# Two attention blocks in one kernel on one Trainium2 core: quotients taken one per score tile, copies given to an engine by its load, and two q chains ahead of k's first

## The chip, the cores and the metric

The kernel runs on one core of one Trainium2 chip. The metric is the device time of one execution in microseconds (us); lower is better. TensorE (PE) does the matmuls, ScalarE (ACT), VectorE (DVE) and GpSimd (POOL) work on their results, and SyncE (SP) issues the transfers (DMAs). Each engine carries out its instructions in program order and waits where an operand is not ready; matmuls write to PSUM, which is held here in banks of 128 x 512 fp32 numbers.

## What is computed

Two blocks, A and B, each with x of 2048 x 640, wqkv of 640 x 1920 and wo of 640 x 640, all bf16; H = 32 heads of Dh = 20. The two outputs stand side by side.

```python
def _A_ref(x, wqkv, wo):                      # W = 256
    q, k, v = ...                             # x @ wqkv, split by heads
    scores = jnp.einsum("bhqd,bhkd->bhqk", q, k) * (Dh ** -0.5)
    mask = (idx[:, None] - idx[None, :] >= 0) & (idx[:, None] - idx[None, :] < W)
    p = _softmax(jnp.where(mask[None, None], scores, -1e9), axis=-1)
    o = jnp.einsum("bhqk,bhkd->bhqd", p, v)
    return o.transpose(0, 2, 1, 3).reshape(B, S, D) @ wo

def _B_ref(x, wqkv, wo):
    phi = lambda t: jnp.where(t > 0, t + 1, jnp.exp(t)) + 1e-6
    pq, pk = phi(q), phi(k)
    kv = jnp.einsum("bhsd,bhse->bhde", pk, v)
    z = jnp.einsum("bhsd->bhd", pk)
    num = jnp.einsum("bhqd,bhde->bhqe", pq, kv)
    den = jnp.einsum("bhqd,bhd->bhq", pq, z)[..., None] + 1e-6
    return (num / den).transpose(0, 2, 1, 3).reshape(B, S, D) @ wo
```

A is attention over a sliding window of 256 positions. B is linear attention, so its sums over the keys are taken once and the queries then go through a merged weight.

## The kernel before

The 2048 rows are handled in four stripes of 512 (s = 0 to 3). A bank is one PSUM buffer `dense`; there are four, used in turn. The scores have a buffer of their own, `S_ps`, of four banks and only one copy.

**Score tiles.** The main loop runs over 76 score tiles, 16 for stripe 0 and 20 for each other stripe. A tile is: the scores of four heads (L742) into S_ps, a tiny ACT instruction on one element (L736), one exp over 128 x 2048 (L760, ACT), and masks by GpSimd (L773, `affine_select`). Two tiles after a group of four heads is complete, `values` multiplies the probabilities with v into a dense bank (L800); VectorE transposes the result (`T`, L811), and later takes the reciprocal of the row sums and normalises (`rest`, L821 and L827). After a stripe's seventh group four DMAs turn the normalised rows for the output product (L841); its last group adds a small transpose on VectorE (L848).

**Fill.** Between the scores of one tile and the next, TensorE gets other matmuls. All of them are in one list `plan`: `at(t0, t1, gen, n)` spreads n banks of a generator over plan times t0 to t1, and `do` places single actions, DMAs among them. The list is sorted by plan time. `take` draws from it: every tile gives `rate` columns of credit, which is (FILL - TAIL + 32 x VALUES) / 76, and a tile with `values` has VALUES columns taken off. So the plan times fix only the order, and the columns fix how many banks go into a tile.

The fill is, in rough order: q, k and v of A (`a_rows`, `a_v`); B's keys with phi (`b_keys`); the sums over B's keys (`b_sums`, `b_kv`); B's queries with phi (`b_q`); the merge of B's values into its weights (`b_merge`, L649); the denominators (`b_den`, L691 on TensorE, L701 and L702 on VectorE); and the output products of both blocks (`a_out`, `b_out`, through `wo_proj`). Before the loop stand the first v chains, the regrouping of the weights of q and k by copies on three engines (`regroup`, L356, L359, L362), and one chain each of q and k.

**What follows a bank.** A chain is five matmuls into one bank. Then either `evac` copies the bank to SBUF, on ACT (L258) or VectorE (L260), or `phi` works on it: exp on ACT (L285), a minimum on VectorE (L290) and a combination on VectorE that reads the bank again (L293). The two VectorE steps are put into `later`, and are issued two banks on or after the next scores, so a phi bank stays taken until then. DMAs that read a result go through `soon(fn, n)`, which issues them n banks later; `settle()` issues all that are waiting. All of them go through SyncE's one queue.

**B's queries.** `b_q(s)` makes five phi banks. After each, a DMA transpose brings it to rows by tokens (`tok`, L679). `b_den(s)` multiplies all five phi tiles with the key sums. A quotient (`quotients`, L714, VectorE) divides 128 rows of `tok` by their denominators, and a DMA transpose (L718) brings them into `oT_B[s]`, which lives in a buffer named `xA`; `b_out(s)` reads it. `divide(t0, t1, s)` places a stripe's four quotients in the plan.

**Who copies.** Where the caller names no engine, `evac` chooses. Before and after the main loop it takes VectorE and ACT by turns. In the loop `spare` holds ACT's allowance in columns: it is raised by 1200 a tile, up to 1200; a copy of n columns goes to ACT if the allowance is at least n, and takes n + 160 off; each phi exp takes 672 off. What ACT has no allowance for goes to VectorE.

Of the kernel before, what the change touches and what calls it, by code (L numbers as in the profile page):

```python
# [20 lines left out]
SB = 512  # L21
TPS = SB // P

FILL = 398440
TAIL = 13000

VALUES = 2200
SPARE = 1200
COPY = 160

# [58 lines left out]
def kernel(  # L91
# [150 lines left out]
            posts.pop(0)[1]()  # L242


    spare = [None]

    def evac(dst, src, n=SB, to=None):

        if to is None:
            to = "D"  # L250
            if spare[0] is None:
                turn[0] += 1
                to = "AD"[turn[0] % 2]
            elif spare[0] >= n:
                spare[0] -= n + COPY
                to = "A"
        if to == "A":
            nc.scalar.activation(out=dst, in_=src, func=ACT.Copy)  # L258
        else:
            nc.vector.tensor_copy(out=dst, in_=src)  # L260

    turn = [0]

    def bank(wide=False):
        flush(begun[0] - 2)
# [15 lines left out]
    def phi(dst, src, view=lambda t: t[:], then=None):  # L281


        e = ep.tile([P, SB], BF16, name="e")
        nc.scalar.activation(out=view(e), in_=src, func=ACT.Exp)  # L285
        if spare[0] is not None:
            spare[0] -= SB + COPY

        def rest():
            nc.vector.tensor_scalar(  # L290
                out=e[:], in0=e[:], scalar1=1e-6, scalar2=1.0 + 1e-6, op0=ALU.add, op1=ALU.min
            )
            nc.vector.scalar_tensor_tensor(  # L293
                out=dst, in0=src, scalar=0.0, in1=view(e), op0=ALU.max, op1=ALU.add
            )
            if then is not None:
                then()

        later.append((begun[0], rest))
# [361 lines left out]
    pq_of, tok_of, rden_of = {}, {}, {}  # L661

    def b_q(s):
        xt = xB[NS + s]
        pq = pqp.tile([P, KT, SB], BF16, name="phi")
        pq_of[s] = pq
        tok = rp.tile([P, TPS, D], BF16, name="tok")
        tok_of[s] = tok
        for c in range(KT):
            ps = bank()  # L670
            yield from chain(
                ps[:],
                lambda kt: w_sb["B"][:, kt, c * P : (c + 1) * P],
                lambda kt: xt[:, kt, :],
                SB,
            )

            def to_tokens(c=c):
                nc.sync.dma_start_transpose(out=tok[:, :, c * P : (c + 1) * P], in_=pq[:, c, :])  # L679

            phi(pq[:, c, :], ps[:], then=lambda fn=to_tokens: soon(fn, 2))
            yield End(SB)

    def b_den(s):

        flush()
        ps = bank()
        dv = ps[:, 0 : TPS * H].rearrange("p (t h) -> p t h", h=H)
        for tb in range(TPS):
            for c in range(KT):  # L690
                nc.tensor.matmul(  # L691
                    dv[:, tb, GH * c : GH * c + NHC],
                    lhsT=pq_of[s][:, c, tb * P : (tb + 1) * P],
                    rhs=zk[:, c, :, 0],
                    start=(tb == 0 and c == 0),
                    stop=(tb == TPS - 1 and c == KT - 1),
                    skip_group_check=True,
                )
        rden = dp.tile([P, TPS, H, 1], F32, name="rden")
        rden_of[s] = rden  # L700
        nc.vector.tensor_scalar_add(out=rden[:, :, :, 0], in0=dv, scalar1=1e-6)  # L701
        nc.vector.reciprocal(out=rden[:], in_=rden[:])  # L702
        yield End(TPS * KT * 64)

    def quotients(s):


        def one(tb):
            settle()
            if tb == 0:  # L710
                oT_B[s] = xp.tile([P, KT, SB], BF16, name="xA")
            v = tok_of[s][:, tb, :]
            vh = v.rearrange("p (h e) -> p h e", e=DH)
            nc.vector.tensor_tensor(  # L714
                out=vh, in0=vh, in1=rden_of[s][:, tb, :, :].to_broadcast([P, H, DH]), op=ALU.mult
            )
            out = oT_B[s][:, :, tb * P : (tb + 1) * P]
            soon(lambda: nc.sync.dma_start_transpose(out=out, in_=v), 1)  # L718

        return [(one, tb) for tb in range(TPS)]  # L720

    def b_out(s):
        settle()
        yield from wo_proj(w_sb["B"], D, oT_B[s], s, D)

# [6 lines left out]
    def scores(s, parts, selects):  # L732
        S_ps = sps.tile([P, 4, SB], F32, name="S_ps")
        p_all = pp.tile([P, 4 * SB + 2], BF16, name="p")
        p = p_all[:, 0 : 4 * SB].rearrange("p (j q) -> p j q", j=4)
        nc.scalar.activation(out=p_all[0:1, 4 * SB : 4 * SB + 1], in_=ident[0:1, 0:1], func=ACT.Copy)  # L736

        def product(g, kb, k0, k1, q0, n, col, step):
            kt = k_pad[kb // TPS]
            ko = (kb % TPS) * P  # L740
            for j in range(4):
                nc.tensor.matmul(  # L742
                    columns(S_ps[k0:k1], j, col, n, step),
                    lhsT=kt[32 * j : 32 * j + DH, g, ko + k0 : ko + k1],
                    rhs=q_pad[s][32 * j : 32 * j + DH, g, q0 : q0 + n],
                    start=True,
                    stop=True,
                    tile_position=(32 * j, k0),
                )

        for g, rel, q0, n, col, step in parts:
            if rel == "M":
                own = key(s, q0 // P)
                product(g, own, 0, HALF, q0, n, col, step)

                far = own - 2 if own >= 2 else own
                product(g, far, HALF, P, q0 + (HALF if own >= 2 else 0), n, col, step)
            else:
                product(g, key(s, rel), 0, P, q0, n, col, step)
        nc.scalar.activation(out=p, in_=S_ps[:], func=ACT.Exp, scale=scale)  # L760
        low = None
        if any(kind == "M" for kind, _, _ in selects):
            low = pl_.tile([P, 4, LOW], BF16, name="plow")
        for kind, c0, n in selects:

            v = p[:, :, c0 : c0 + n].rearrange("p j (b q) -> p j b q", q=HALF)
            if kind == "M":
                lv = low[:, :, c0 - LOW : c0 - LOW + n].rearrange("p j (b q) -> p j b q", q=HALF)
                jobs = [(lv, v, 1, 0), (v, v, -1, -HALF - 1)]
            else:  # L770
                jobs = [(v, v, 1, HALF) if kind == "D" else (v, v, -1, -1)]
            for dst, src, sgn, base in jobs:
                nc.gpsimd.affine_select(  # L773
                    out=dst,
                    in_=src,
                    pattern=[[0, 4], [0, n // HALF], [sgn, HALF]],
                    compare_op=ALU.is_ge,
                    fill=0.0,
                    base=base,
                    channel_multiplier=-sgn,  # L780
                )
        return p, low

    def values(s, g, held):
# [24 lines left out]

        T = tp.tile([P, SB // 32, 32], F32, name="T")  # L810
        nc.vector.transpose(out=T.rearrange("p b e -> p (b e)"), in_=O_ps[:])  # L811
        if s not in norm_A:
            norm_A[s] = (
                np_.tile([P, SB // 32, P], BF16, name="N"),
# [142 lines left out]


    first_rows = {n: a_rows(n, 0) for n in "qk"}
    for n in "qk":  # L960
        run(banks(first_rows[n], 1))


    plan = []
# [17 lines left out]

        do(t0, t1, [one] * 4)

    def divide(t0, t1, s):
        do(t0, t1, [lambda fn=fn, tb=tb: fn(tb) for fn, tb in quotients(s)])

    for n, t in (("q", 0), ("k", 0.1)):
        at(t - 0.5, t + 3.5, first_rows[n], KT - 1)
        reads_of(t + 5, t + 6, n, 0)  # L990
    for s, tq, tk, tv in ((1, (2.2, 8), (7, 12), (10, 15)), (2, (19, 26), (25, 32), (16, 22)),
                          (3, (36, 41.5), (41, 46), (43, 49))):
# [10 lines left out]
        do(t, t, [lambda s=s: load_tok(s)])  # L1003
    at(40.4, 42, b_kv(), 2)
    do(42.8, 44.8, [lambda c=c: kv_ready(c) for c in range(3)])
    for s, tq, td, tx in ((0, (39.5, 45), 47, (49, 51)), (1, (45, 50), 53.4, (55.5, 58)),
                          (2, (51.5, 56.5), 59.6, (61, 63.5)), (3, (58.2, 62.2), 64, (65.5, 67.5))):
        at(*tq, b_q(s), KT)
        at(td, td + 0.1, b_den(s), 1)
        divide(*tx, s)  # L1010
    at(46.5, 54, b_merge(), 2 * KT)
    for n, s, t0, t1 in (("A", 0, 44.5, 48.5), ("A", 1, 51.5, 55.5), ("B", 0, 55.5, 59.5),
                         ("B", 1, 60.2, 64), ("B", 2, 64.4, 68.2), ("B", 3, 69, 73),
                         ("A", 2, 73, 76)):
        at(t0, t1, (a_out if n == "A" else b_out)(s), KT)
    for n, s, t0, t1 in (("B", 1, 5, 9), ("A", 2, 6, 12), ("B", 2, 14, 18), ("A", 3, 16, 24),
                         ("B", 3, 17, 22)):
# [30 lines left out]
    n_values = NS * NG  # L1048
    rate = (FILL - TAIL + n_values * VALUES) / len(units)
    credit = 0.0  # L1050
    spare[0] = 0
    for i, (s, parts, selects, done) in enumerate(units):
        p = scores(s, parts, selects)
        flush()
# [5 lines left out]
        if ready and ready[0][0] + LAG <= i:  # L1060
# [5 lines left out]
            if last:  # L1066
                flush()
            credit -= VALUES
        spare[0] = min(spare[0] + SPARE, SPARE)
        credit -= take(credit)  # L1070
    spare[0] = None
    while ready:
        take(5500)
        _, at = ready.popleft()
# [36 lines left out]
```

## Time and profile before

| | |
|---|---|
| time, three runs | 270.23, 270.6, 271.66 us; median 270.6 |
| the profiled execution | 270.09 us, span 268.0 |
| TensorE busy | 254.9 us (95%), 4769 matmuls |
| ACT busy | 214.8 us (80%), 293 instructions |
| GpSimd busy | 171.0 us (64%), 211 instructions |
| VectorE busy | 157.1 us (59%), 267 instructions |
| exp of a score tile, L760 | 76 times, 1.87 us |
| copies of a bank on ACT, L258, 512 columns | 0.59 us |
| copies of a bank on VectorE, L260, 512 columns | 0.68 us |
| phi on VectorE, L290 and L293 | 40 times each, 0.63 and 0.69 us |
| quotient, L714 | 16 times, 1.12 us |

The span is the time from the first to the last instruction in the profile. The profile's first part gives each engine's busy time, its second the busy share in 40 slices of 6.7 us, as tenths, with the clock granted to TensorE (PEclk, 9 is 90% or more). The list of waits names the engine and line that waited, what ended the wait, and the total, the count and the longest in us. A timeline line has start, duration, engine, line, operation, output <- input, and a count. A line of the windows' table has the stretch and its length, then busy time (and count) of PE, PEld (weight loads), VectorE, ACT and GpSimd, then the clock, the DMA share and GB/s.

### The profile page before, as it was taken

The numbers are of one execution on the slowest core, as the hardware profiler recorded it, in microseconds if no ns is written. First come the engines' busy times: TensorE is split into PE (matmuls) and PEld (weight loads), VectorE is DVE, ScalarE is ACT, GpSimd is POOL, SyncE is SP. The second block draws the span as 40 slices with busy tenths as digits, with TensorE's granted clock in tenths as the row PEclk, the third lists the DMA queues.
The fourth block names the chain that finished last, engine by engine and source line by source line (L and its number), as shares of the span: only waits on it lengthen the run. The fifth ranks groups of instructions, "written<-read, shape, count | busy, mean of one in ns | idle before, by whom it ended". The sixth has DMA issues, their size and how long they took to land.

```text
span 268.0 us, 10800 instructions
## 1 busy us (share of the span) xinstructions
PE 254.9 (95%) x4769; PEld 143.1 (53%) x4769; DVE 157.1 (59%) x267; ACT 214.8 (80%) x293; POOL 171.0 (64%) x211
## 2 busy tenths in 40 slices
PE   8979999999999999999999999999799999889995
PEld 7524445556556655454476455564345454435573
DVE  1512379566522166776535553667948987996572
ACT  2578988899999979997787989998398888858631
POOL 6216667778775749386666789595654685956600
PEclk9999999999999999999999999999799999999999
DMA  6992369699769982304623594316486857377505
GB/s 198 329 257 98 53 138 191 123 272 187 95 122 261 164 218 46 130 4 86 114 88 96 95 164 117 82 22 166 87 160 104 181 78 159 71 145 124 189 22 186
DMA packets 65507, 36.35 MB, mean 136 GB/s; under 512 B 48181, under 2 KB 64437, under 8 KB 65461
## 3 DMA queue, kind: packets, MB, share of 16 engines
q1 hardware_dynamic: 65461, 35.67, 59.7%
q8 instruction: 37, 0.61, 0.9%
q14 instruction: 9, 0.07, 0.1%
HBM read 14.42 MB, written 9.83 MB: 90 GB/s over the span
## 4 chain that ended last, share of the span: by engine, by line
PE 77%; DVE 7%; DMA 5%; ACT 4%; POOL 3%; issue 2%; SPq 1%; DVEq 0%
PE dense L275 49%; PE dense L542 9%; PE S_ps L742 9%; PE dense L800 8%; DVE tok L714 3%; DMA wA<-in_A_wqkv_dram 2%; POOL p L773 2%; ACT p L760 2%; DVE e L290 2%; DMA xA<-tok 2%; DMA out_dram<-osb 1%; DVE N L827 1%; POOL plow L773 1%; DVE phi L293 1%; ACT wqk L356 1%
## 5 line engine op out<-in xcount | busy, mean ns | idle before, releaser
L773 POOL TENSOR_SCALAR_AFFINE_SELECT p<-p 128x512 bf16<-128x512 bf16 (+1 forms) x152 | 122.5, 815 | 73.5 <-ACT p L760 67.3
L760 ACT ACTIVATE p<-S_ps 128x2048 bf16<-128x2048 f32 x76 | 142.3, 1872 | 25.9 <-PE S_ps L742 25.1
L275 PE MATMUL dense<-xA,wqk 128*128 128x512 bf16 x200 | 50.1, 380 | 1.3 <-ACT wqk L356 1.3
L290 DVE TENSOR_SCALAR e<-e 128x512 bf16<-128x512 bf16 x40 | 25.0, 625 | 32.4 <-ACT e L285 22.0
L773 POOL TENSOR_SCALAR_AFFINE_SELECT plow<-p 128x1024 bf16<-128x1024 bf16 x32 | 38.8, 1211 | 2.2
L811 DVE STREAM_TRANSPOSE T<-dense 128x512 f32<-128x512 f32 x32 | 22.7, 710 | 27.7 <-PE dense L800 27.5
L275 PEld LDWEIGHTS <-xA 128*128 128x128 bf16 x320 | 26.3, 98 | 19.0 <-issue 2.1
L742 PE MATMUL S_ps<-qpad,kpad 20*64 20x64 bf16 (+3 forms) x1728 | 35.2, 214 | 0.7 <-ACT kpad L258 0.7
L742 PEld LDWEIGHTS <-kpad 20*64 20x64 bf16 (+1 forms) x1728 | 17.4, 100 | 31.6 <-issue 25.8
L800 PE MATMUL dense<-p,vA 128*32 128x64 bf16 (+2 forms) x1152 | 27.3, 226 | 2.2 <-DVE phi L293 1.7
L275 PEld LDWEIGHTS <-wqk 128*128 128x128 bf16 x200 | 18.0, 98 | 21.0 <-issue 3.2
L293 DVE SCALAR_TENSOR_TENSOR phi<-dense,e 128x512 bf16<-128x512 f32 x40 | 27.7, 692 | 1.6
L275 PE MATMUL dense<-wA,xA 128*128 128x320 bf16 x160 | 27.1, 301 | 0.4 <-DMA wA<-in_A_wqkv_dram 0.4
L275 PE MATMUL dense<-xB,wB 128*128 128x512 bf16 x100 | 26.4, 384 | 0.6 <-ACT p L736 0.6
L275 PE MATMUL dense<-wB,xB 128*128 128x512 bf16 (+1 forms) x160 | 26.6, 300 | 0.0
L800 PEld LDWEIGHTS <-vA 128*32 128x32 bf16 x1664 | 22.6, 97 | 7.1 <-issue 3.1
L275 PE MATMUL dense<-wB,xA 128*128 128x512 bf16 (+1 forms) x160 | 25.3, 300 | 0.5 <-DMA xA<-tok 0.4
L275 PE MATMUL dense<-wo,oT 128*128 128x512 bf16 (+2 forms) x160 | 25.2, 304 | 0.4 <-ACT p L736 0.4
L285 ACT ACTIVATE e<-dense 128x512 bf16<-128x512 f32 x40 | 23.8, 597 | 1.9 <-PE dense L275 1.6
L542 PE MATMUL dense<-phi,tok 128*128 128x512 bf16 (+1 forms) x160 | 24.9, 300 | 0.0
L258 ACT ACTIVATE osb<-dense 128x512 bf16<-128x512 f32 (+1 forms) x26 | 14.6, 571 | 9.9 <-PE dense L275 9.9
L827 DVE TENSOR_TENSOR N<-T,recA 128x320 bf16<-128x320 f32 (+1 forms) x28 | 19.0, 678 | 1.0
(66 smaller groups left out, 228.0 us busy)
## 6 DMA issues: line engine op xcount, KB each, us to landing
out_dram<-osb SPq DMA_DIRECT2D x7, 640.0 KB
x_scr<-xB SPq DMA_DIRECT2D x4, 640.0 KB
tok<-in_B_x_dram SPq DMA_DIRECT2D x4, 640.0 KB
xB<-x_scr SPq DMA_DIRECT2D x4, 640.0 KB
wB<-in_B_wqkv_dram SPq DMA_DIRECT2D x3, 800.0 KB
q_scr<-qpad SPq DMA_DIRECT2D x16, 60.0 KB
k_scr<-kpad SPq DMA_DIRECT2D x16, 60.0 KB
qpad<-q_scr SPq DMA_DIRECT2D x16, 60.0 KB
```

Source lines behind the costliest of these rows:

```text
L258: nc.scalar.activation(out=dst, in_=src, func=ACT.Copy)
L275: nc.tensor.matmul(dst, lhsT=lhs(kt), rhs=rhs(kt), start=(kt == 0), stop=(kt == KT - 1))
L285: nc.scalar.activation(out=view(e), in_=src, func=ACT.Exp)
L290: nc.vector.tensor_scalar(out=e[:], in0=e[:], scalar1=1e-6, scalar2=1.0 + 1e-6, op0=ALU.add, op1=ALU.min)
L293: nc.vector.scalar_tensor_tensor(out=dst, in0=src, scalar=0.0, in1=view(e), op0=ALU.max, op1=ALU.add)
L542: nc.tensor.matmul(out, lhsT=lhs(x, pk)[:, tb, :], rhs=rhs(pk, tb), start=(i == 0), stop=(i == len(blocks) - 1),)
L742: nc.tensor.matmul(columns(S_ps[k0:k1], j, col, n, step), lhsT=kt[32 * j : 32 * j + DH, g, ko + k0 : ko + k1], rhs=q_pad[s][32 * j : 32 * ...
L760: nc.scalar.activation(out=p, in_=S_ps[:], func=ACT.Exp, scale=scale)
L773: nc.gpsimd.affine_select(out=dst, in_=src, pattern=[[0, 4], [0, n // HALF], [sgn, HALF]], compare_op=ALU.is_ge, fill=0.0, base=base, chan ...
L800: nc.tensor.matmul(O_ps[32 * j : 32 * (j + 1), q0 : q0 + n], lhsT=v_flat[kb // TPS % 3][:, at + j * HV : at + j * HV + 32], rhs=columns(p, ...
L811: nc.vector.transpose(out=T.rearrange("p b e -> p (b e)"), in_=O_ps[:])
L827: nc.vector.tensor_tensor(out=dst[:, :, at : at + b - a], in0=T[:, :, a - lo : b - lo], in1=r[:].to_broadcast([P, SB // 32, b - a]), op=AL ...
```

## The change

Three things change, and the numbers of the plan with them.

- Of A's stripe 0, two chains of q and one of k run ahead of the loop instead of one and one. FILL falls by 2560, the columns of one chain.
- `evac` takes ACT if its load is below VectorE's by this count plus 600, else VectorE. The counts are raised by every copy (its columns + 160), by the exp of a tile (ACT 2080), by phi (ACT 672, VectorE 1300), `values` (VectorE 1500), a denominator (1200) and a quotient (1000); at the end of a tile each falls by 3000, but not below 0. The rule holds for the copies outside the loop too.
- The four quotients of a stripe go into a queue after its denominator. A tile without `values` issues one; a tile with `values` issues one only if more than two are queued. `b_q(s)` first empties the queue of the stripes up to s - 2, and `b_out(s)` up to s.

In the plan the denominators come earlier (47, 53.4, 59.6, 64 become 46.3, 51.8, 58.7, 63.2), and A's output of stripe 2 changes places with B's of stripe 3.

```diff
-FILL = 398440
+FILL = 395880
 VALUES = 2200
-SPARE = 1200
+TILE = 3000
 COPY = 160
+AHEAD = 600
...
-    spare = [None]
+    load = {"A": 0, "D": 0}
+
+    def add_load(a=0, d=0):
+        load["A"] += a
+        load["D"] += d
+
+    def pass_tile():
+        for e in load:
+            load[e] = max(load[e] - TILE, 0)
 
     def evac(dst, src, n=SB, to=None):
         if to is None:
-            to = "D"
-            if spare[0] is None:
-                turn[0] += 1
-                to = "AD"[turn[0] % 2]
-            elif spare[0] >= n:
-                spare[0] -= n + COPY
-                to = "A"
+            to = "A" if load["A"] < load["D"] + AHEAD else "D"
+        load[to] += n + COPY
...
         nc.scalar.activation(out=view(e), in_=src, func=ACT.Exp)
-        if spare[0] is not None:
-            spare[0] -= SB + COPY
+        add_load(a=SB + COPY, d=1300)
...
     def b_q(s):
+        quotient(s - 2)
...
         rden_of[s] = rden
+        add_load(d=1200)
...
+    quotients_due = deque()
+
+    def quotient(s=None):
+        while quotients_due and (s is None or quotients_due[0][0] <= s):
+            at, tb, fn = quotients_due.popleft()
+            fn(tb)
+            if s is None:
+                break
...
         def one(tb):
             settle()
+            add_load(d=1000)
...
-        return [(one, tb) for tb in range(TPS)]
+        quotients_due.extend((s, tb, one) for tb in range(TPS))
 
     def b_out(s):
+        quotient(s)
         settle()
...
         nc.scalar.activation(out=p, in_=S_ps[:], func=ACT.Exp, scale=scale)
+        add_load(a=2080)
...
         nc.vector.transpose(out=T.rearrange("p b e -> p (b e)"), in_=O_ps[:])
+        add_load(d=1500)
...
-    for n in "qk":
-        run(banks(first_rows[n], 1))
+    for n, c in (("q", 2), ("k", 1)):
+        run(banks(first_rows[n], c))
...
-    for n, t in (("q", 0), ("k", 0.1)):
-        at(t - 0.5, t + 3.5, first_rows[n], KT - 1)
+    for n, t, c in (("q", 0, 3), ("k", -0.4, 4)):
+        at(t - 0.5, t + 3.5, first_rows[n], c)
...
-    for s, tq, td, tx in ((0, (39.5, 45), 47, (49, 51)), (1, (45, 50), 53.4, (55.5, 58)),
-                          (2, (51.5, 56.5), 59.6, (61, 63.5)), (3, (58.2, 62.2), 64, (65.5, 67.5))):
+    for s, tq, td in ((0, (39.5, 45), 46.3), (1, (45, 50), 51.8), (2, (51.5, 56.5), 58.7),
+                      (3, (58.2, 62.2), 63.2)):
         at(*tq, b_q(s), KT)
         at(td, td + 0.1, b_den(s), 1)
-        divide(*tx, s)
+        do(td + 0.2, td + 0.2, [lambda s=s: quotients(s)])
     for n, s, t0, t1 in (("A", 0, 44.5, 48.5), ("A", 1, 51.5, 55.5), ("B", 0, 55.5, 59.5),
-                         ("B", 1, 60.2, 64), ("B", 2, 64.4, 68.2), ("B", 3, 69, 73),
-                         ("A", 2, 73, 76)):
+                         ("B", 1, 60.2, 64), ("B", 2, 64.4, 68.2), ("A", 2, 69, 73),
+                         ("B", 3, 73, 76)):
...
             credit -= VALUES
-        spare[0] = min(spare[0] + SPARE, SPARE)
+            if len(quotients_due) > 2:
+                quotient()
+        else:
+            quotient()
         credit -= take(credit)
-    spare[0] = None
+        pass_tile()
```

More of the change, by code (lines that the diff above doesn't have):

```diff
@@ L260, in evac @@
             nc.vector.tensor_copy(out=dst, in_=src)
-    turn = [0]
     def bank(wide=False):
@@ L983, in reads_of @@
         do(t0, t1, [one] * 4)
-    def divide(t0, t1, s):
-        do(t0, t1, [lambda fn=fn, tb=tb: fn(tb) for fn, tb in quotients(s)])
-    for n, t in (("q", 0), ("k", 0.1)):
-        at(t - 0.5, t + 3.5, first_rows[n], KT - 1)
+    for n, t, c in (("q", 0, 3), ("k", -0.4, 4)):
+        at(t - 0.5, t + 3.5, first_rows[n], c)
         reads_of(t + 5, t + 6, n, 0)
@@ L1050 @@
     credit = 0.0
-    spare[0] = 0
     for i, (s, parts, selects, done) in enumerate(units):
```

## The prediction

> **What bounds the kernel now.** I read the page's slices, the windows, the starts of the 76 score tiles in the timeline (ACT L760, numbered 0 to 75), TensorE's waits, and then the timelines of the bad places. The slices:
>
> ```profile
> span 268.0 us, 10800 instructions
> PE   8979999999999999999999999999799999889995
> DVE  1512379566522166776535553667948987996572
> ACT  2578988899999979997787989998398888858631
> PEclk9999999999999999999999999999799999999999
> ```
>
> The span is 268.0 us, the profiled execution 270.09 (2.1 around it), the median of the runs 270.6, so 0.5 above the profiled one. The table of windows, for the two stretches (engine busy us, then clock):
>
> ```profile
> 17.00:184.00 167.00, 166.44 (x3291) 91.41 (x3284) 89.07 (x156) 148.74 (x201) 118.13 (x139) 1.00 0.58 126
> 184.00:251.00 67.00, 61.07 (x1169) 32.76 (x1167) 53.35 (x82) 53.11 (x73) 44.50 (x48) 0.97 0.66 132
> 188.00:192.00 4.00, 2.42 (x98) 1.70 (x98) 3.97 (x6) 1.88 (x1) 2.27 (x3) 0.76 0.47 86
> 192.00:196.00 4.00, 4.00 (x55) 1.75 (x54) 3.74 (x8) 2.14 (x4) 1.82 (x2) 0.82 0.53 108
> ```
>
> From 17 to 184 TensorE is idle for 0.6 us. Exp of tile 0 starts at 17.22 and of tile 56 at 184.84: 2.99 us a tile, TensorE's own pace. Tile 75's starts at 250.44: 65.6 us for 19 tiles that would take 56.9 at that pace. So **8.7 us are lost after 184**: 4.8 in tiles 56 to 60 (201.61 - 184.84 - 4 x 2.99), 3.9 after. VectorE is near full there in most slices. One place in its timeline shows the pattern:
>
> ```profile
> 185.98 0.69 DVE L293 SCALAR_TENSOR_TENSOR phi<-dense,e 128x512 bf16<-128x512 f32 x1
> 186.59 3.20 DVE L714 TENSOR_TENSOR tok<-tok,rden 128x640 bf16<-128x640 bf16 x3
> 189.72 0.48 DVE L260 CAST wB<-dense 128x320 bf16<-128x320 f32 x1
> 190.12 0.81 DVE L714 TENSOR_TENSOR tok<-tok,rden 128x640 bf16<-128x640 bf16 x1
> ```
>
> And from the list of waits (total us, times, longest):
>
> ```profile
> PE dense L800 <- DVE wB L260: 1.6, 1, 1.6
> PE dense L275 <- ACT wqk L356: 1.3, 1, 1.3
> ```
>
> All four quotients of a stripe (512 rows) stand in one tile; a bank's copy (L260) is queued behind three of them, and TensorE waits 1.6 us for that bank. The second wait is the one before k's first chain, at 13.5.
>
> **Part 1: q's second chain first.** TensorE stands idle from 13.54 to 14.84 until ACT's 1.86 us copy of k's weights (L356) ends. A chain of five 512-column matmuls costs 5 x 216 ns = 1.08 us in a row and fits in. Its copy goes to ACT after L356 (ends 14.7 + 0.6), before the exp at 17.2; k's first goes to VectorE (0.69 instead of 0.60). The first scores stay at 16.8, and the tiles have 2,560 columns less: **-1.1 us** (bounds -1.1 and 0, if the first scores slip).
>
> **Part 2: who copies.** I followed the planner's arithmetic in order, bank by bank: columns per tile (395880 - 13000 + 32 x 2200)/76 = 5,964 (5,998 before), plan items by time, loads as `add_load` counts them. For the kernel before this gives 89 ACT and 35 VectorE copies, as L258 and L260 have without the four each of the last output. Changed: 46 and 78. So 43 copies go from ACT (0.595 us at 512 columns, 0.436 at 320) to VectorE (0.685, 0.487): ACT about 25 us lighter, VectorE 28 heavier. Summed by mean durations (exp 2.07 with its small L736; phi 0.625 + 0.692; T 0.71; the rest of values 0.98; quotient 1.12; den 1.23):
>
> tiles 0-41: ACT 123 to 107, VectorE 68 to 86 us in 125;
> tiles 42-55: ACT 43 to 39, VectorE 26 to 37 in 42;
> tiles 56-75: ACT 59 to 55, VectorE 60 to 59 in 60.
>
> Up to tile 41 I cost it at nothing: no tile gives VectorE over 3.5 us, and its backlog, summed tile by tile, stays under 0.5, where four banks let it be some 2 us late (before, it reaches 1.1 in these tiles, and TensorE does not stop there); the one wait of the stretch (0.6 at 43.6, behind phi) probably goes: **-0.4** (0 to -0.6). In tiles 42-55 VectorE rises to 88%, with 4.2 and 4.9 us in tiles 48 and 50: **+0.5** (0 to 1.5).
>
> The copies read PSUM: L260 takes 0.65 to 0.69 us at 512 columns wherever it stands, while L290, all in SBUF, takes from 0.28 to 1.24 beside POOL. [...]
>
> **Part 3: one quotient a tile.** Before, tile 56 has 9.1 us of VectorE work (norm, two phi, four quotients, two copies), 71 has 4.1. Changed, stripe 0's quotients stand in tiles 52, 53, 54, 56; 1's in 58, 59, 61, 63; 2's in 66 to 69; 3's in 70, 71, 73, 74. The largest tiles are 58 (5.3) and 69 (5.0); the backlog peaks at 2.8 to 3.0 us in 56 to 59 and 4.5 in 69, against 6.1 and 5.4.
>
> But the denominators move up too: den1 from tile 59 to 56, den2 from 66 to 64, den3 from 70 to 69. In tile 56 I stepped through the queues (0 = its first score matmul). TensorE comes to den1 (L691) at 2.4. It needs the stripe's last phi, which waits on ACT for exp (till 2.3 to 2.6) and its own 0.6, and on VectorE behind quotient 0.3 and two copies: done at 3.5 to 4.6. **New TensorE wait: 1.1 to 2.2 us**, with everything later in program order behind it. Then quotient 1.0 (tile 58) needs the last tok transpose (L679). SP is one queue in order:
>
> ```profile
> 185.54 5.98 SPq L841 DMA_TRANSPOSE oT<-N  x4
> 191.62 1.21 SPq L679 DMA_TRANSPOSE tok<-phi  x1
> 198.01 0.55 SPq L903 DMA_DIRECT2D xB<-x_scr  x1
> 198.65 1.21 SPq L718 DMA_TRANSPOSE xA<-tok  x1
> 199.98 5.20 SPq L679 DMA_TRANSPOSE tok<-phi  x2
> ```
>
> Changed, 5.98 + 1.2 + 1.2 + 0.6 lie ahead of that transpose: issued at 8 to 9, landed 2.4 to 4.0 later (completion marks of L679), so 10.4 to 13. VectorE is there at 8.5 and stands 2 to 4 us, with copies of merge 3.1 and oA1.1 and phi bq2.0 queued behind; TensorE, four banks on, waits 0.5 to 3.1 for them. Together tiles 56-60 then lose 1.6 to 5.2 instead of 4.8; I take 3.5, near the middle: **-1.3** (-3.2 to +0.4).
>
> Tiles 61-75: den3 waits for its phi 0.6 (0.8 before, at 234.9), values of tile 70 some 1.0 for a bank (1.1 before), and the 0.5 us wait for stripe 2's transposes at 238.6 goes, since its first quotient is a tile earlier. I take 2.3 lost for 3.9: **-1.6** (-3.4 to +1).
>
> **Part 4: A 2's output before B 3's.** Same columns. The last transposes, issued at 240.0 to 245.6, get two more tiles: nothing off, the end after 251 is TensorE's own.
>
> **Sum:** -1.1 - 0.4 + 0.5 - 1.3 - 1.6 = -3.9. Profiled 270.09 - 3.9 = 266.2; against the median 270.6 - 3.9 = **266.7 us**.
>
> **The half clock.** At 188 to 196 the clock column is 0.76 and 0.82: 0.24 x 4 + 0.18 x 4 = 1.7 us lost, after waits of 0.4, 0.6 and 1.65 us in a row; single ones of 1.5 (13.2) and 1.1 (232.7) cost none. It is in the 4.8, and I assume it gone. [...]
>
> **Rivals.** (a) The queue clears it, 0.22: the last transpose lands at 10.4, phi comes early, L290 and L714 run at their quick ends. 2.5 of 8.7 stay: -6.2 - 1.5 = -7.7, 263 us. For: VectorE has 59 us for 60 by durations that POOL already stretches. Against: the SP rows.
> (b) The new waits eat it, 0.13: tiles 56-60 lose 5.2 and 61-75 4.4, the middle 0.5: 0.4 + 0.5 + 0.5 - 1.5 = -0.1, 270.5.
> (c) Slower, 0.24: a denominator too close behind its phi. Place: L691 in tiles 56, 64 and 69. From a wait of about 1.7 us on, the half clock joins: 2.1 + 1.7 = 3.8 each, 11.4 for 8.7, with the middle's +0.5 and part 1: 270.6 + 2.7 + 0.5 - 1.1 = 272.7. For: den3 waits 0.8 already, and VectorE fills up. Against: den2 has half a us to spare by my steps.
> Forecast: 0.41. That the change does not do what it says has its share in (b): "by load" mostly sends copies to VectorE, 18 for 11 in tiles 56-75.
>
> **Range and chances.** A measurement here can tell about 0.5%, 1.35 us. From (a)'s middle to (c)'s: 262.5 to 273.0. Faster by more: all of (a) and nearly all of the forecast, 0.62; within: (b) and the edge of the forecast, 0.14; slower: (c), 0.24.
>
> **What would show it.** L258 with 50 and L260 with 82 executions; ACT about 190 us busy, VectorE 185. Exp of tile 0 at 17.2 and of 56 about 1 us earlier. A TensorE wait at L691 for phi L293 of 1 to 2 us near 185, then VectorE idle at L714 for a tok transpose. No 3.2 us row of three quotients, clock 1.00 from 188 to 196. Wrong if tiles 0-41 take over 3.0 us each, if L714 never waits, or if the clock drops more than once.

## The result and the profile after

The changed kernel takes 273.0 us in the median of its runs (271.03 to 274.12) against 270.65 (269.02 to 274.32) for the kernel before: a ratio of 1.0088, 95% interval 1.0067 to 1.0109. It is 0.9% slower; 266.7 us and "faster" were forecast. The profiled execution has a span of 271.1 us, 3.0 more than before (271.08 against 268.05). Executions that took over 1.5% longer than the fastest of their kernel are left out of the ratios, and of the median of e10 below (270.87 and 271.05 us, two of its six; with them it would be 268.29).

Ahead of the experiments, the starts of the 76 exps give the account by stage. All numbers are us from the profiled executions; four tiles at TensorE's pace take 11.97.

| kernel | start to tile 56 | 56-60 | 60-66 | 66-75 | after | span |
|---|---|---|---|---|---|---|
| before | 184.84 | 16.77 | 18.64 | 30.19 | 17.60 | 268.0 |
| changed | 183.41 | 24.65 | 17.82 | 27.66 | 17.53 | 271.1 |

The change gains 1.4 us up to tile 56 and 3.35 from tile 60 to 75, and **loses 7.9 in four tiles**. The page of the changed kernel shows the hole in its slices (6.8 us each):

```profile
span 271.1 us, 10748 instructions
PE   8989999999999999999999999996639999999995
DVE  0535787687545667755458676888343978997652
ACT  3656889888867889886678877885607798977742
PEclk9999999999999999999999999999957999999999
```

Three slices of TensorE fall to 6, 6 and 3; VectorE falls to 3 and 4 in the last two of them; the clock goes down to 5 and 7. In the deepest part no engine is short of time: from 196 to 200 TensorE, VectorE and ACT all stand. The table of windows of the same kernel shows that (stretch and length, then busy us and counts of PE, PEld, VectorE, ACT and GpSimd, then clock, DMA share, GB/s):

```profile
17.00:182.00 165.00, 161.22 (x3248) 90.84 (x3278) 110.57 (x198) 132.61 (x160) 119.55 (x138) 1.00 0.62 128
182.00:210.00 28.00, 18.23 (x298) 8.78 (x299) 14.65 (x26) 14.17 (x22) 10.16 (x13) 0.82 0.56 116
196.00:200.00 4.00, 0.00 (x0) 0.00 (x0) 0.08 (x1) 0.00 (x0) 1.31 (x2) 0.61 0.63 179
200.00:204.00 4.00, 2.80 (x14) 0.73 (x14) 3.37 (x6) 0.77 (x1) 0.00 (x0) 0.50 0.23 48
```

Some matmul records are missing from this trace (4722 of 4769), so the 161.22 of the first row is a little low; the starts of the tiles are not touched by that. TensorE's waits, the three that stand in the hole:

```profile
PE dense L277 <- DVE wB L264: 7.2, 1, 7.2
...
PE dense L693 <- DVE phi L294: 1.9, 2, 1.5
...
PE dense L693 <- DVE wB L264: 0.7, 1, 0.7
```

The 7.2 us are a wait for a bank whose copy (L264) is queued on VectorE. VectorE's timeline shows behind what:

```profile
191.38 0.71 DVE L866 STREAM_TRANSPOSE oT<-Nr 128x512 bf16<-128x512 bf16 x1
199.92 0.83 DVE L729 TENSOR_TENSOR tok<-tok,rden 128x640 bf16<-128x640 bf16 x1 [7.83 <-DMA tok<-phi]
200.66 0.48 DVE L264 CAST wB<-dense 128x320 bf16<-128x320 f32 x1
```

VectorE is done at 192.09 and stands 7.83 us at stripe 1's first quotient (L729 is L714 of the kernel before), until stripe 1's last transpose to `tok` lands; the copy that TensorE needs is the next instruction. The transpose itself stands late in SP's queue (L681 was L679, L859 was L841):

```profile
182.66 1.84 SPq L391 DMA_DIRECT2D kpad<-k_scr  x3
184.61 6.05 SPq L859 DMA_TRANSPOSE oT<-N  x4
190.77 2.34 SPq L681 DMA_TRANSPOSE tok<-phi  x1
193.21 1.22 SPq L733 DMA_TRANSPOSE xA<-tok  x1
194.53 0.54 SPq L921 DMA_DIRECT2D xB<-x_scr  x1
195.16 1.20 SPq L681 DMA_TRANSPOSE tok<-phi  x1
```

It is issued at 195.16 and lands at 199.80. What tiles 56-60 take over their pace is 24.65 - 11.97 = 12.7 us. Three things make up 12.4 of it: the denominator's two waits at L693, 2.2 (0.7 for a bank's copy and 1.5 for a phi; the other 0.4 of the 1.9 in the list is stripe 3's), the bank, 7.2, and the half clock. That one lasts from 196.88 to 207.12; TensorE works in it from 201.20 on, so it costs half of 5.9, 3.0 us. The remaining 0.3 us were not taken apart.

### The profile page after: what moved, and what is told of

Same layout as the page of the kernel before. It is cut to its first block, busy times and chain, and to the rows that moved or that the text cites. A ratio compares the mean times of both kernels' runs of the same rounds, so it can differ in the third digit from the quotient of the medians.

```text
span 271.1 us, 10748 instructions
## 1 busy us (share of the span) xinstructions
PE 250.3 (92%) x4722; PEld 143.2 (53%) x4769; DVE 175.8 (65%) x310; ACT 197.9 (73%) x250; POOL 172.0 (63%) x211
## 4 chain that ended last, share of the span: by engine, by line
PE 81%; DVE 8%; DMA 4%; issue 3%; SPq 2%; ACT 1%; DVEq 0%; ACTq 0%
PE dense L277 52%; PE S_ps L758 10%; PE dense L543 9%; PE dense L817 9%; DMA wA<-in_A_wqkv_dram 2%; DMA tok<-phi 2%; DVE e L291 2%; DVE tok L729 2%; DVE phi L294 2%; DVE T L828 1%; ACT wqk L357 1%; PE dense L622 1%; PE dense L693 1%; PE dense L650 0%; SPq L733 0%
## 5 line engine op out<-in xcount | busy, mean ns | idle before, releaser
L277 PE MATMUL dense<-xA,wqk 128*128 128x512 bf16 x185 | 49.2, 380 | 1.5 <-issue 1.0
L291 DVE TENSOR_SCALAR e<-e 128x512 bf16<-128x512 bf16 x40 | 21.1, 528 | 13.7 <-ACT e L287 13.4
L817 PE MATMUL dense<-p,vA 128*32 128x64 bf16 (+2 forms) x1152 | 26.6, 223 | 0.3 <-DVE osb L264 0.3
L277 PE MATMUL dense<-wB,xB 128*128 128x512 bf16 (+1 forms) x155 | 25.3, 297 | 0.8 <-DVE phi L294 0.3
L277 PE MATMUL dense<-wo,oT 128*128 128x128 bf16 (+2 forms) x153 | 24.6, 304 | 0.6 <-issue 0.3
L543 PE MATMUL dense<-phi,tok 128*128 128x128 bf16 (+1 forms) x153 | 23.7, 296 | 0.9 <-issue 0.8
L277 PE MATMUL dense<-wB,xA 128*128 128x128 bf16 (+1 forms) x152 | 23.5, 295 | 0.6 <-issue 0.5
L264 DVE CAST osb<-dense 128x512 bf16<-128x512 f32 (+1 forms) x24 | 15.6, 652 | 11.2 <-PE dense L277 9.7
L729 DVE TENSOR_TENSOR tok<-tok,rden 128x640 bf16<-128x640 bf16 x16 | 16.6, 1040 | 7.8 <-DMA tok<-phi 7.8
```

Source lines behind the costliest of these rows:

```text
L277: nc.tensor.matmul(dst, lhsT=lhs(kt), rhs=rhs(kt), start=(kt == 0), stop=(kt == KT - 1))
L291: nc.vector.tensor_scalar(out=e[:], in0=e[:], scalar1=1e-6, scalar2=1.0 + 1e-6, op0=ALU.add, op1=ALU.min)
L543: nc.tensor.matmul(out, lhsT=lhs(x, pk)[:, tb, :], rhs=rhs(pk, tb), start=(i == 0), stop=(i == len(blocks) - 1),)
L729: nc.vector.tensor_tensor(out=vh, in0=vh, in1=rden_of[s][:, tb, :, :].to_broadcast([P, H, DH]), op=ALU.mult)
L817: nc.tensor.matmul(O_ps[32 * j : 32 * (j + 1), q0 : q0 + n], lhsT=v_flat[kb // TPS % 3][:, at + j * HV : at + j * HV + 32], rhs=columns(p, ...
```

## The experiments

**The theory**: the two early places of stripe 1, of its denominator (51.8) and of its quotients right behind it, cost all of the loss, through SP's queue; the rest of the change is a gain. **The rivals**: VectorE is overloaded by the copies that the load rule gives it; the half clock, and not the DMA, is what is lost; the queue of quotients is a loss as such. The medians, with the ratio to runs of the kernel before beside them:

| run | us | ratio (95%) | 56-60 | 66-75 | span |
|---|---|---|---|---|---|
| e1_den1_quot1_late | 262.47 | 0.9718 (0.9681-0.9756) | 13.38 | 27.77 | 260.3 |
| e2_quot1_late | 265.25 | 0.9849 (0.9784-0.9914) | 14.57 | 27.71 | 262.0 |
| e3_turns_after_tok | 265.82 | 0.9845 (0.9801-0.9888) | 16.56 | 27.64 | 263.6 |
| e4_part1_alone | 265.11 | 0.9818 (0.9771-0.9865) | 15.03 | 27.48 | 262.8 |
| e5_e1_without_part2 | 262.96 | 0.9722 (0.9657-0.9787) | 13.66 | 27.73 | 261.3 |
| e6_part1_and_part2 | 263.73 | 0.9746 (0.9679-0.9813) | 13.53 | 28.50 | 261.7 |
| e7_e1_without_part4 | 266.18 | 0.9845 (0.9767-0.9924) | 13.29 | 31.38 | 264.0 |
| e8_part1_stripe1_early | 274.86 | 1.0174 (1.0094-1.0254) | 26.41 | 27.03 | 272.7 |
| e9_fill_alone | 272.37 | 1.0074 (1.0041-1.0108) | 14.16 | 31.15 | 268.8 |
| e10_reload_later | 266.88 | 0.9874 (0.9817-0.9931) | 21.01 | 27.65 | 267.9 |

The part ahead of the first exp is the same in the changed kernel, e1, e2, e3, e7 and e10, and yet exp of tile 0 starts anywhere from 17.14 to 17.97 us. So much of a difference between two spans can be the start alone; the stages are free of it.

### Stripe 1 later, nothing else (e1)

```diff
-... (1, (45, 50), 51.8), ...
+... (1, (45, 50), 53.4), ...
-        do(td + 0.2, td + 0.2, [lambda s=s: quotients(s)])
+        tx = 54.3 if s == 1 else td + 0.2
+        do(tx, tx, [lambda s=s: quotients(s)])
```

> The changed kernel with stripe 1's denominator back at plan time 53.4 (tile 59) and its quotients from 54.3 (first in tile 61, as before the change). Theory: the loss sits in tiles 56 to 60 alone, 12.7 us over the pace: 2.5 us at the denominator L693, 7.3 us for a bank behind the quotient that waits for a tok transpose, and 3.0 us of half clock. All three go: 273.0 - 12.7 + about 1.5 of new small waits = about 262 us (260 to 264), clock 1.00, no wait of VectorE for a DMA over 1 us. Rival (VectorE carries 43 copies more and is late for that reason): banks stay late wherever the quotients stand, 269 to 273.

It takes 262.47 us, 10.5 under the changed kernel and 2.8% under the kernel before; it is the fastest of all that were run. Its page:

```profile
span 260.3 us, 10797 instructions
...
DVE  0435687778654568666645867688899898978652
...
PEclk9999999999999999999999999999999999999999
```

The clock stays whole and VectorE has no hole. SP's queue has hardly changed:

```profile
194.72 0.54 SPq L921 DMA_DIRECT2D xB<-x_scr  x1
195.35 6.67 SPq L681 DMA_TRANSPOSE tok<-phi  x4
```

The transpose that the changed kernel waited for is issued here at 195.35, even 0.2 later; only VectorE comes to the quotient after it has landed. So the transfer never was too slow for the work, it was asked for too early. VectorE has the same 310 instructions as in the changed kernel (177.1 us busy there against 175.8): the rival of an overloaded VectorE falls.

### Only the quotients later (e2)

The second half of that edit alone, with 54.0 for 54.3; the denominator stays at 51.8.

> The changed kernel with stripe 1's denominator where the change put it (tile 56) and only its quotients later, from plan time 54.0 (first in tile 60). Theory: the denominator's wait of 2.5 us stays, the bank's 7.3 and the half clock's 3.0 go: 273.0 - 10.3 + 0.5 = about 263 us (262 to 266), 1 to 3 us above the run with both late. Rival (the denominator's wait is what lets the clock fall and holds everything behind it): half clock stays, 268 to 271.

265.25 us. Tiles 56-60 lose 2.6 over their pace. TensorE's list has the denominator's waits of the changed kernel, to the tenth (L693: 1.9 in two, the longest 1.5, and one of 0.7). VectorE's wait at the quotient is gone. By the medians the quotients' place is worth 273.0 - 265.25 = 7.8 us, the denominator's 265.25 - 262.47 = 2.8. In the profiled execution, at the whole clock, the denominator's place costs only 1.2 in tiles 56-60 (14.57 against 13.38); of the 1.7 between the spans 0.5 is a later start (first exp at 17.97 against 17.43). Much of the rest of the 2.8 goes with the clock: the four timed executions have spans of 262.0, 263.1, 263.9 and 265.7 at mean clocks of 1.000, 0.994, 0.994 and 0.987, while those of e1 are all at 0.999 or 1.000. So this kernel loses clock in some executions and not in others. That it loses it at the denominator's waits, which e1 does not have there, is likely, but only the execution with the whole clock has a trace.

### The queue in front of the transpose (e3)

Quotients and denominator stay early; the four transposes of A's output of stripe 2 (L859), which take 6 us of SP's time, are held until after the transposes to `tok`:

```diff
-                soon(turn_all, 2)
+                if s == 2:
+                    turn_due.append(turn_all)
+                else:
+                    soon(turn_all, 2)
...
+    do(52.05, 52.05, [lambda: turn_due.pop()()])
```

> The changed kernel; the four transposes that turn stripe 2's normalised rows (L859, 6 us of SyncE's queue) are issued behind stripe 1's last tok transpose instead of ahead of it. Denominator and quotients as in the change. Theory (SyncE's queue is what the quotient waits for): the tok transpose is issued at about tile 56's start + 5 instead of + 12.3 and lands at about + 8 to 9.5 instead of + 17.0; VectorE waits under 1 us, TensorE's 7.3 us and the half clock go: about 263 us (262 to 266). Rival (the 640 KB reload of x ahead of it sets the landing, 4.6 us after the issue): most of the wait stays at 3 us or more, 267 to 271.

265.82 us. SP and VectorE:

```profile
189.56 1.21 SPq L681 DMA_TRANSPOSE tok<-phi  x1
190.82 5.88 SPq L860 DMA_TRANSPOSE oT<-N  x4
```

```profile
DVE tok L729 <- DMA tok<-phi: 2.3, 1, 2.3
```

The same transpose is issued 5.6 us sooner, VectorE stands 2.3 instead of 7.8, and TensorE's bank wait is gone. With the transposes no longer in front, 5.5 us of the wait go. The time came as expected, the landing did not: the transpose lands at 195.14, 5.58 us after its issue and 11.7 after the start of tile 56, where 8 to 9.5 were expected. The reload of x (L925 here, 640 KB) is still issued 0.6 us ahead of it, and the four held transposes now follow right behind; this run does not separate the two. One stretch of half clock is left, at 190.2, without any DMA wait ahead of it; it follows the denominator's waits.

### Part 1 alone (e4)

The kernel before with `FILL = 395880`, `(("q", 2), ("k", 1))` and `(("q", 0, 3), ("k", -0.4, 4))`.

> The kernel before with part 1 alone: two chains of q and one of k ahead of the loop, FILL less by 2560. Theory: the chain fits into the 1.3 us in which TensorE waits for k's weights; first exp at 17.2 +- 0.1, every later tile about 1.1 us earlier: -1.1, 269.5 us (ratio 0.996). Rival: the end does not follow, since the later waits of tiles 56 to 60 and 70 to 72 take other shapes when the bank order shifts by one: anything from -3 to +2.

265.11 us: 5.1 off the time where part 1 had been costed at -1.1. From the first exp to tile 56 the gain is 0.98, as costed. The rest is not in the edit's own place: 1.74 come in tiles 56-60 and 2.71 in 66-75. With 2,560 columns less, the plan's items fall into other tiles. One of them can be seen. Of the three quotients in a row of the kernel before, one is now issued before the tile with the phis, the denominators and the copies:

```profile
183.62 1.32 DVE L714 TENSOR_TENSOR tok<-tok,rden 128x640 bf16<-128x640 bf16 x1
```

The half clock of the kernel before (0.76 and 0.82 at 188 to 196) is gone in this execution too. That the broken row is the reason is not shown: 11 of the 27 executions of the kernel before that were timed beside the experiments have the whole clock (0.999 or 1.000) as well.

### Fewer columns a tile alone (e9)

The kernel before with `FILL = 395880` and nothing else: each tile gets 34 columns less, and no chain is taken out. This is not e4's shift. In e4 the chain is gone from in front of the late items, which come sooner: stripe 0's first quotient starts 0.2 us ahead of the exp of tile 56, where the kernel before has it 1.8 behind. In e9 they come later: stripe 0's last quotient starts 7.1 us behind that exp, where the kernel before has 5.3.

> The kernel before with FILL less by 2560 and nothing else: each tile gets 34 columns less, one chain is left over for after the loop, and the places of late items move by up to one tile. No work is taken out or hidden. Theory (part 1 alone gave 5.1 us and not 1.1 because the late items came to stand otherwise, its first quotient in tile 55 and not 56): places alone move the time by some us, here either way, 268 to 274, without a change up to tile 50 of more than 1 us. Rival (the 4 us belong to q's chain ahead of k's): 270.6 + up to 1.

272.37 us, slower by 0.7%. The profiled execution is the fastest of its runs (span 268.8 at a clock of 1.000; most others have 0.987), so the stages tell only of 0.8 of the 2.4 us. In them tiles 56-60 gain 2.6, and three other stages lose 0.9 to 1.0 each: from the first exp to tile 56, 66-75, and after tile 75, where the columns left over are done. So 34 columns a tile move stages by 1 to 3 us, in either direction. Whether e4's own shift gives the rest of its gain is argued and not shown: e9 moves the items the other way. Which of the moved items makes the 2.71 us of 66-75 in e4 was not followed further, and stays open.

### The load rule alone and taken out (e6, e5)

e6 adds `add_load`, `pass_tile` and the new choice in `evac` to e4. e5 is e1 with the old allowance (`spare`, 1200 a tile).

> The kernel before with parts 1 and 2: q's second chain first, and the copies by load; quotients, denominators and output order as before. Against part 1 alone (265.1 us). Theory: the quotients still stand three and four in a tile, VectorE now has more copies there and the banks behind them come later: 265.5 to 268. Rival (the load rule sends the copies round the burst): 262 to 264.

> The run with stripe 1's denominator and quotients late (262.5 us), but with the old rule for the copies (ACT's allowance of 1200 columns a tile); queue of quotients, output order and part 1 kept. Theory: the choice of copier is not what moved the time; with the quotients spread, neither engine is late by more than the banks allow: 262.5 +- 1.5. Rival (the copies by load carry the gain): ACT is again some 25 us heavier and TensorE waits for banks behind exp: 265 to 268.

e6 takes 263.73, 1.4 less than e4; e5 takes 262.96, 0.5 more than e1. In both pairs the single times of the two kernels overlap. In the spans it is 1.1 and 1.0. So the rule is worth some 0.5 to 1.4 us, which four times of each kernel do not settle further. In both pairs it gains ahead of tile 56 (0.5 and 1.0 us from the first exp on), and it gains most where quotients still stand in a row: tiles 56-60 take 13.53 in e6 against 15.03 in e4. It is no gain everywhere: e6 is 1.0 slower than e4 in tiles 66-75 (28.50 against 27.48), where e5 and e1 agree (27.73 and 27.77).

### The old order of the outputs in the best kernel (e7)

```diff
-... ("A", 2, 69, 73), ("B", 3, 73, 76)):
+... ("B", 3, 69, 73), ("A", 2, 73, 76)):
```

> The run with stripe 1's denominator and quotients late (262.5 us), with the outputs in the old order: B's stripe 3 before A's stripe 2. Theory: B's last product then comes two to three tiles after its first quotient and waits for the transposes, as tiles 71 and 72 did before the change (1.7 and 1.0 us over the pace): 263.5 to 266. Rival (nothing depends on the order): 262 to 263.

266.18 us, 3.7 slower than e1, all of it in tiles 66-75. TensorE's list of waits:

```profile
PE dense L277 <- DMA xA<-tok: 3.4, 2, 1.9
```

In the old order B's output of stripe 3 reads its transposed quotients as soon as they can be there, twice too soon: both waits stand between the exps of tiles 74 and 75, which are 6.37 us apart.

### Stripe 1's early times without the queue (e8)

e4 with `(1, (45, 50), 53.4, (55.5, 58))` turned into `(1, (45, 50), 51.8, (52, 54))`: no load rule, no queue of quotients, the old order of outputs.

> The kernel before with part 1, and of the rest only this: stripe 1's denominator at plan time 51.8 and its quotients from 52 to 54, which puts the denominator into tile 56 and the first quotient into tile 58, as the change has them. Old copies, no queue, old order. Theory: these places alone bring the loss: a denominator wait of 2 to 3 us, then VectorE stands 7 us or more for the last tok transpose and the clock halves: 265.1 + 9 to 13 = 274 to 278. Rival (it takes the heavier VectorE of part 2 as well): 266 to 270.

274.86 us, 9.75 over e4, with the same picture as the changed kernel:

```profile
PE dense L275 <- DVE osb L260: 6.3, 1, 6.3
PE dense L691 <- DVE phi L293: 3.5, 1, 3.5
```

```profile
DVE tok L714 <- DMA tok<-phi: 6.9, 1, 6.9
```

So the two early times are enough to make the loss, without the queue, the load rule or the new order. With e1 that settles the theory from both sides.

### The transfer in flight in front (e10)

The last transpose took 4.64 us from issue to landing in the changed kernel, and a reload of 640 KB (L921) was issued 0.6 us before it. e10 is the changed kernel with the place of that reload moved from 51.2 to 54.5.

> The changed kernel with the 640 KB reload of x for stripe 3 (L921) issued some tiles later, behind stripe 1's last tok transpose. Theory (the queue ahead and the transfers in flight both hold the transpose): it is issued 0.6 us earlier and lands 2.4 to 2.7 us after its issue instead of 4.6, so VectorE waits about 5 us instead of 7.8, TensorE about 4.5 instead of 7.3; with a window of half clock less: 273.0 - 2.8 - 1 = about 269 us (267.5 to 270.5). Rival (the landing is set by the transposes ahead alone): 272 to 273.

266.88 us (266.04 to 269.56). The profiled execution is the longest of these four, with a span of 267.9 where the others have 264.3 to 265.3, so the trace explains only 3.2 of the 6.1 us by which the median is shorter. SP, then the last transpose from issue to landing in the changed kernel and in e10 (from the list of the chain that ended last), then VectorE:

```profile
194.52 1.22 SPq L681 DMA_TRANSPOSE tok<-phi  x1
```

```profile
195.16 4.64 DMA tok<-phi
194.52 2.43 DMA tok<-phi
```

```profile
197.07 1.67 DVE L729 TENSOR_TENSOR tok<-tok,rden 128x640 bf16<-128x640 bf16 x1 [3.86 <-DMA tok<-phi]
```

It lands at 196.95, 2.43 us after its issue. VectorE stands 3.9 us (5 expected), TensorE 3.2 at the bank (4.5 expected). So 2.85 us of the landing were the reload's: 0.64 by its place in the queue, 2.2 by what it has in flight (tile 56 starts 0.4 later here and the transpose ahead takes 0.3 less, which nearly cancel). The other 1.1 us of the shorter wait are VectorE's, which comes to the quotient that much later. Two stretches of half clock of 3.41 us stand in this trace, one after the denominator's waits (from 189.38) and one after the bank (from 199.62). As with e3, a part of the queue is cured and a part of the loss stays.

## Why the prediction was wrong

**The step that failed is a term of part 3**: the wait of stripe 1's first quotient for its transpose. The prediction had named the wait, the queue that causes it and the copies behind it, and e1 and e8 show that this is where the time goes. It sized it at 2 to 4 us for VectorE and 0.5 to 3.1 for TensorE; measured are 7.83 and 7.2. With the half clock below, the term of -1.3 us for tiles 56-60 came out at +7.9 (24.65 against 16.77), while the other stages gained more than was forecast: 1.4 against 1.0 up to tile 56, 3.35 against 1.6 after tile 60. Counted from the start of tile 56 (its first score matmul, 182.83), the transpose was to be issued at 8 to 9 and to land at 10.4 to 13. It was issued at 12.3 and landed at 17.0. By the working's own figures (5.98 + 1.2 + 1.2 + 0.6) the issue would be at 9.0. In the kernel before SP is done with its reads of `kpad` at 183.97, 0.4 us ahead of that tile's first score matmul (184.39):

```profile
182.88 1.09 SPq L390 DMA_DIRECT2D kpad<-k_scr  x2
```

The 3.3 us by which the issue was missed, and the landing:

- The sum began as if SP were free at the start of the tile. The transposes of L859 began at 184.61, 1.8 us later: three reads of `kpad` (1.84 us) stand ahead, which the sum left out. In front of them the changed kernel has a transpose that the change itself moved ahead, of one of stripe 0's quotients (L733, 1.2 us, issued at 180.75); in the kernel before the first of these is issued at 193.48. That it is what delays the reads was not tested.
- The transpose to `tok` ahead of it took 2.34 us and not 1.2. Another 0.4 us are gaps of 0.1 between issues.
- The landing took 4.64 and not 2.4 to 4.0, because the 640 KB reload was in flight (e10: 2.43 without it in flight).

**The half clock, assumed gone, came back** because of that wait: 3.0 us. The prediction had it only in a rival, behind denominators. That rival (c) had the right sign and the wrong place. Stripe 1's denominator does wait 2.2 us, for a copy and a phi (1.1 to 2.2 forecast, for the phi alone; its place is worth 2.8 by the medians of e2 and e1, 1.2 in tiles 56-60 at the whole clock), but stripe 3's waits 0.4 and stripe 2's not at all in the list, where (c) priced each at 3.8. So tiles 56-60 lost 12.7, where 3.5 were forecast with 5.2 as the worst. That the total still came to (c)'s 272.7 and the range's upper end, 273.0, is luck: a loss in one place that no line of the working had so large, less gains elsewhere that were not forecast so large either. The wait of 1.7 us from which (c) let the half clock join is shown by no run: the waits of 0.7 and 1.5 here cost a step of half clock in the traces of e3 and e10 and none in those of e2 and the changed kernel.

The other steps:

- **Part 1** was right where it was made: exp of tile 0 at 17.14 (17.2 forecast; 17.14 to 17.97 over the kernels with this start) and the gain from there to tile 56 with e4, 0.98 of 1.1. That fewer columns move every later item, and that this is worth several us (e4, e9), was not in the prediction at all.
- **Part 2** was right in its counts and signs: 50 and 82 copies as forecast, ACT 197.9 us busy (190 forecast), VectorE 175.8 (185). Tile 56 starts 1.43 us earlier (about 1 forecast). The +0.5 for the fuller VectorE in tiles 42-55 did not show; the rule gains 0.5 to 1.4. Two of its readings are off a little: in the kernel before L260 takes 0.63 to 0.69 us at 512 columns, and L290 0.23 to 1.25 (0.23 to 0.29 in the eight executions that meet no GpSimd instruction).
- **Part 3 after tile 60**: 3.35 us gained where 1.6 were forecast. But e4 without any queue has 46.46 us for tiles 60-75, e6 47.38, and the changed kernel 45.48. Only 1.0 to 1.9 of the gain can be the queue's and the new order's; the rest is there with part 1 alone.
- **Part 4** was costed at nothing, with no price for the lost cover. e7 gives that price: 3.7 us. The queue spreads stripe 3's quotients out to the end: the last one is issued 7.4 us before the exp of tile 75 in the kernel before (243.01 and 250.44) and 2.7 us before it in the changed one (250.87 and 253.54). The old order of the outputs would have had TensorE wait for them. Queue and order belong together.

**The clock in the hole**: TensorE stopped at 194.04, and the clock was half from 196.88 to 207.12. These 10.24 us are three times the 3.41 that the half clock lasts in the kernel before, from 190.04 on. The fall came 2.84 us after the stop; in the 3.41 us ahead of it TensorE was busy for 0.57. In the three times 3.41 us of half clock it was busy for 0, 2.51 and 3.41, and then the clock was whole again. What sets the fall and the return is not shown.

## What to carry to other kernels

When a step moves ahead of a transfer it reads, write down the issuing queue from its last idle moment, with every issue in it and at the longest duration of its row, and add what large transfer is in flight when it is issued; then ask which instruction stands behind the waiting one. The same change with two of its plan times moved by 1.6 and 2.3 went from 0.9% slower to 2.8% faster, so test the times one stripe at a time before a scheme is judged. In a plan whose items are dealt out by columns, removing a few columns moves everything behind them: price that by a run of the removal alone.

## What the runs showed of the hardware

**In three traces the clock fell behind 3.4 us in which TensorE was busy for 1.5 to 1.9, and in two the same waits did not cost it.** In the kernel before, the changed one and e10 the changes of the clock lie whole multiples of a step of 3.413 us apart: in the kernel before it is half for one step and then whole for 22 (75.09 us, 193.46 to 268.55, behind the work), in the changed one half for three and whole for 19 (64.85 us, 207.12 to 271.97, behind the work); in e10 the two falls are three apart (189.38 and 199.62). In the trace of e3 TensorE is busy 1.90 of the 3.40 us from 186.8 to 190.2, and the clock halves from 190.2 to 193.6; in the kernel before it is busy 1.51 of 3.40 from 186.6 to 190.0, and the clock halves from 190.0 on; in e10 it is busy 1.55 of 3.41 up to 189.38, and the clock halves from there. In e3 and e10 the whole second wait of the denominator, 1.5 us, falls into that step. In the profiled executions of e2 and of the changed kernel the same waits of the denominator (0.7 and 1.5) cost no clock. There the steps, if they are counted back by 3.41 us from the next fall of the clock (196.88 in the changed kernel, 262.44, behind the work, in e2), part in the middle of the second wait (at 186.64 in 186.15 to 187.66, and at 187.35 in 187.02 to 188.52), and TensorE is busy 2.2 to 2.3 us of the step on either side. So where the waits fall in the steps fits all five traces; that it decides was not tested by itself. The busy time of a step alone does not decide: in e7 TensorE is busy only 1.47 us of the step from 242.50 to 245.91, and the clock stays whole.

Among the executions of e2 the mean clock falls by 0.006 to 0.007 at a time (1.000, 0.994 twice, 0.987); 0.0065 x 262 = 1.7 us is half of one step of 3.41. By this estimate one kernel pays none, one or two of these steps from run to run.

**A transpose lands late behind a large transfer.** With a 640 KB reload issued 0.6 us ahead, the last transpose to `tok` of stripe 1 took 4.64 us from issue to landing in the changed kernel and 5.58 in e3, where four more transposes follow it; without the reload it took 2.43 (e10). The issue itself keeps SP busy for 1.2 us in some places and 2.0 to 2.3 in others: behind the four transposes of L859 it takes 2.34 in the changed kernel and 2.14 in e1, but 1.21 behind the same four in the kernel before (L841), and 2.05 in e3 with none of them ahead. What makes the difference is not shown.
